# Every on-chip tile that a DMA reads or writes begins at a multiple of 256 bytes

## The chip, the core and the metric

The kernel runs on one core of one Trainium2 chip. The metric is the device time of one execution in microseconds (us). The kernel before takes 676.39 us, the median of three runs (676.08 to 677.17).

## What is computed

A hashed attention is followed by two dense expert layers. Each query and key falls into one of 64 buckets by the signs of six projections; a query sees only the keys of its own bucket.

```python
# q, k, v: [2, 8, 768, 64]; proj: [64, 6]
bucket = sum(((x @ proj) > 0) * 2**arange(6))           # for x = q and x = k
scores = where(q_bucket == k_bucket, q @ k.T / 8, -1e9)
attn   = softmax(scores) @ v                             # -> x: [1536, 512]
h = maximum(maximum(x @ w1, x @ w2), x @ w3)             # w1, w2, w3: [512, 768]
x = h @ w_out                                            # [768, 512]
g = x @ w_in                                             # [512, 2048]
out = where(g > 0, g, exp(minimum(g, 0)) - 1) @ w_out2   # [2048, 512]
```

Inputs and output are float32. TensorE multiplies float16 parts: each operand is split into a high and a low half, and a product is three matmuls (high by high, high by low, low by high).

## The kernel before

The work is cut into 24 units (two batches, three chunks of 256 queries, four pairs of heads), a unit into four tiles of 128 queries by 768 keys: 96 attention tiles. One tile goes through all engines. TensorE makes the scores (line 609), VectorE their row maximum (612), ScalarE the exponential into `P` (617), ScalarE, VectorE or GpSimd the high half and then GpSimd or VectorE the low half into `hl` (623, 625, 628). A DMA transpose from the SyncE queue turns `hl` into `PT` (630), 128 partitions of 1,536 elements of two bytes, and TensorE multiplies `PT` by the values (639 to 641). The result is divided, split into `xn` (661, 662) and transposed by another DMA into `xT` (665), from which the first expert layer starts. So each attention tile has one DMA transpose of 384 KB in its path, and there are 96 of them, with 12 smaller ones for `xT`.

Other DMAs load the inputs (`rawq`, `rawk`, `rawv`), the weights (`raww`, `raw2`) and store the output (`ot`); plain copies inside the chip bring half of the transposed queries and keys to other partitions (`qb<-qa`, `kb<-ka`, line 414) and add the bucket bits (`qb<-btq`, `kb<-btk`, line 461).

The order of the work is not found while the kernel runs. A graph of operations is built, and the string `ORDER` holds the sequence in which they are issued and the engine of each. Each engine executes its instructions in that sequence, and semaphores hold one back until its data are there. All tiles stand in pools that are laid out one after the other along the memory of a partition: `const`, `tiny` (small columns), `w13o` (weights of the first expert layer), `xp`, `hp`, `attn` (all tiles of the attention), and from the other end `wpre` (weights as loaded). When the attention is done its pool closes and `w2p` and `mp` (second expert layer) take its place; `x1p` takes that of `wpre`. Where a tile of a new pool lies over a tile of the old one, its first writer waits for the old tile's last user.

Where a tile begins is the sum of the sizes before it. The table in the section on the change gives the places.

Of the kernel before, what the change touches and what calls it, by code (L numbers as in the profile page):

```python
# [11 lines left out]
F32 = mybir.dt.float32  # L12
F16 = mybir.dt.float16
# [157 lines left out]
def lsh_attention_moe_kernel(ctx: ExitStack, tc: tile.TileContext, q, k, v, proj,  # L171
# [3 lines left out]
    NB = proj.shape[1]  # L175
# [11 lines left out]
    KM = DM // 128  # L187
    FM = DFF // 128
    F2 = DFF2 // 128
    NCH = B * NH  # L190
# [20 lines left out]
    const = ctx.enter_context(tc.tile_pool(name="const", bufs=1))  # L211
    tiny = ctx.enter_context(tc.tile_pool(name="tiny", bufs=2))
# [4 lines left out]
    at = g2.enter_context(tc.tile_pool(name="attn", bufs=1))  # L217
    gw = ctx.enter_context(ExitStack())
    wpre = gw.enter_context(tc.tile_pool(name="wpre", bufs=1, side="right"))
# [3 lines left out]
    late = {}  # L223
# [4 lines left out]
    def ring(pool, shape, tag, bufs, dt=F32, ordered=False):  # L228
        p = pool if callable(pool) else (lambda: pool)
        return g.buf(p, list(shape), dt, tag, bufs, ordered)  # L230

    def tn(n, tag, bufs, dt=F32):
        return ring(tiny, [128, n], tag, bufs, dt)
# [12 lines left out]
    tinyc = const.tile([128, 1], BF16, name="tinyc")  # L246
    flip = const.tile([128, 2], F32, name="flip")
    vts_ = [at.tile([128, 2, NS, VP], F16, name=f"vt{i}") for i in range(NP)]

    def emit_const():  # L250
        V.memset(ones, 1.0)
        V.memset(ones3, 1.03125)
        make_identity(nc, ident)
        A.activation(out=junk[:, 0:1], in_=ones[:, 0:1], func=AF.Square)

        V.memset(capc, 2.0 ** (2 * (62 + TQK - CAPQK) - 127 - 7))
        V.memset(pbt, 0.0)

        G.memset(tinyc, 2.0 ** -126)

        for j, (x, y) in enumerate(((1.0, -1.0), (0.0, 32768.0))):
            G.memset(flip[:, j:j + 1], x)
            G.affine_select(out=flip[:, j:j + 1], in_=flip[:, j:j + 1], compare_op=ALU.is_ge, fill=y,
                            base=QT * 4 * NB - 1, pattern=[[0, 1]], channel_multiplier=-1)

        for t in vts_:
            G.memset(t[:, :, :, D:D + 1], 1.0)
# [96 lines left out]
    def plan_qk(kind, b, p, hf, u, prio):  # L364
# [4 lines left out]
        nt = heads * n  # L369
# [3 lines left out]
        nb = QB if kind == "q" else NP  # L373
        raw = ring(at, [128, heads, n, D], "raw" + kind, 1 if kind == "q" else 2, ordered=True)
        nat = ring(at, [128, heads * n, 2, D], "nat" + kind, 1, F16, True)
        bits = ring(at, [128, NB * (2 if kind == "q" else 1), nt], "bits" + kind, 1, F16)
        ta = ring(at, [128, heads, n, 128], kind + "a", nb, F16, True)
        tb = ring(at, [128, heads, n, 128], kind + "b", nb, F16, True)
        acc, s, inv = tn(1, "acc" + kind, 2), tn(1, "s" + kind, 2), tn(1, "inv" + kind, nb + 1)
# [176 lines left out]
    w13 = wp.tile([128, FM, 3, 2, 512], F16, name="w13")  # L556
    wot = wp.tile([128, FM, 2, 512], F16, name="wot")
    swm = const.tile([128, 2, FM], F32, name="swm")
    osc = const.tile([128, 2], F32, name="osc")
    osm = const.tile([128, 2], F32, name="osm")  # L560
    omg = const.tile([128, 2], F32, name="omg")
    wosc = const.tile([128, FM], F32, name="wosc")
    wops = []

    def plan_w13(f, prio):
# [102 lines left out]


    x1T, x1acc, sx = {}, {}, {}  # L670

    def mm3(o, lh, rh, n):

        for kk in range(n):
            for pi, (x, y) in enumerate(((0, 0), (0, 1), (1, 0))):
                PE.matmul(o, lh(kk, x), rh(kk, y), start=(kk == 0 and pi == 0), stop=(kk == n - 1 and pi == 2))  # L676

    def plan_moe1(c, p0, dp):
# [32 lines left out]
        if c % 2 == 0:  # L711
            x1T[c // 2] = ring(lambda: late["x1p"], [128, KM, 2, 2 * NQ], "x1T", NCH // 2, F16)
        xs = slice(c % 2 * NQ, (c % 2 + 1) * NQ)
        x1acc[c] = const.tile([128, KM // 2], F32, name=f"x1acc{c}")
        sx[c] = const.tile([128, 2], F32, name=f"sx{c}")
        ch = tn(2, "ch", 2)
        pr = p0 + 18 * dp
        x2 = sumsq([bufcol(hacc, f) for f in range(FM // 2)], pr, also=[ch])
# [138 lines left out]
    for u in range(NU):  # L857
        c, p = divmod(u, NP)
        b, hf = divmod(c, NH)
        t0 = UL * u  # L860
        if hf == 0:
            plan_qk("k", b, p, hf, u, t0 - LQ)
        if p % 2 == 0:
            plan_qk("q", b, p, hf, u, t0 - LQ)
        if hf == 0:
            plan_v(b, p, t0 - LV)
        if u == NP - 1 or (hf == 0 and p == NP - 1):
            plan_vmin(b, t0 - LV)
# [20 lines left out]
            g.after(ld, sops[t])  # L889

    def close_w(e):
        gw.close()
        late["x1p"] = ctx.enter_context(tc.tile_pool(name="x1p", bufs=1, side="right", reuse_waits="tile"))

    g.after(op({"N": 0}, close_w, wr=["x1p"], prio=0.0 + 282.28), *wops)
    for c in range(NCH):
        if c % NH == 0:
            plan_sh(c // NH, (c + 1) * CS + LM + 18 * DM1)
        plan_moe1(c, (c + 1) * CS + LM + CM * c * 16, DM1)

    def close_attn(e):
        g2.close()
        late["w2p"] = ctx.enter_context(tc.tile_pool(name="w2p", bufs=1, side="right", reuse_waits="tile"))
        late["mp"] = ctx.enter_context(tc.tile_pool(name="mp", bufs=2, reuse_waits="tile"))
        late["ps_t"] = ctx.enter_context(tc.tile_pool(name="ps_t", bufs=1, space=PSUM, reuse_waits="tile"))
        late["ps_out"] = ctx.enter_context(tc.tile_pool(name="ps_out", bufs=2 * QT, space=PSUM, reuse_waits="tile"))

    g.after(op({"N": 0}, close_attn, wr=["w2p"], prio=0.0 + 767.79), *attn_ops)
    D2 = 51.9327
    M2 = NCH * CS + LM + 23 * DM1  # L910
    for c in range(NCH):
        plan_moe2_x(c, M2 - LM + c)
    f = 0
# [42 lines left out]
```

## Time and profile before

| | |
|---|---|
| median of 3 runs | 676.39 us |
| the profiled execution | 679.45 us |
| its span, first to last instruction | 677.6 us |
| TensorE matmuls busy | 621.6 us (92% of the span) |
| VectorE busy | 534.9 us (79%) |
| ScalarE busy | 443.5 us (65%) |
| GpSimd busy | 257.2 us (38%) |
| DMA packets | 201258, 167776 of them under 512 bytes |

Busy times are of one execution. The page cuts the span into 40 slices of 17 us; a digit is the busy share of a slice in tenths. The share of the DMA engines is the time of the packets that start in a stretch over 16 engines' time in it; packets overlap, so it can pass 100%.

### The profile page before, as it was taken

What the parts mean: (1) busy time and instruction counts of PE and PEld (TensorE: products, weight loads), DVE (VectorE), ACT (ScalarE), POOL (GpSimd) and SP (SyncE); (2) the same over time, 40 slices, a digit from 0 to 9 for tenths busy, and PEclk for the clock granted to TensorE, in tenths of its full rate; (3) what the DMA queues carried; (4) which work ended last, traced back from release to release, by engine and by line L of the source; (5) the groups of instructions that cost most, each with busy time, mean ns of one, the idle gap of its engine ahead of it and who ended that gap; (6) DMA issues with size and microseconds to landing.
All of it is one profiled execution on the core that took longest, in us unless ns stands there. A gap on an engine that the chain in (4) does not pass through costs nothing.

```text
span 677.6 us, 15392 instructions
## 1 busy us (share of the span) xinstructions
PE 621.6 (92%) x5838; PEld 421.2 (62%) x5838; DVE 534.9 (79%) x1478; ACT 443.5 (65%) x824; POOL 257.2 (38%) x244
## 2 busy tenths in 40 slices
PE   4776767999999999999999999999999999999997
PEld 4554446788878888777778886644444444444443
DVE  6898979999988778686965787877768887768655
ACT  4879977899677667767643688786665655633342
POOL 0344656476465556667542011133221112311111
PEclk9967657999999999999989999999999999999999
DMA  8999999999999977988977752321211000000003
GB/s 265 254 231 216 250 229 200 212 185 158 183 161 160 141 145 134 167 131 156 136 137 135 227 169 94 126 65 60 71 57 62 28 35 1 1 0 1 33 31 125
DMA packets 201258, 87.58 MB, mean 129 GB/s; under 512 B 167776, under 2 KB 195680, under 8 KB 201184
## 3 DMA queue, kind: packets, MB, share of 16 engines
q1 hardware_dynamic: 192810, 77.23, 55.8%
q10 hardware_dynamic: 8374, 9.37, 4.9%
q8 instruction: 46, 0.75, 0.5%
q14 instruction: 28, 0.23, 0.1%
HBM read 38.80 MB, written 3.15 MB: 62 GB/s over the span
## 4 chain that ended last, share of the span: by engine, by line
PE 62%; DMA 14%; DVE 9%; ACT 4%; issue 2%; POOL 2%; SPq 1%; ACTq 0%; DVEq 0%; POOLq 0%
PE mo L676 35%; PE out L804 18%; DMA PT<-hl 10%; PE s L609 4%; DMA raww<-in_moe_w_dram 2%; DVE m L612 2%; PE o L639 2%; PE o L640 1%; PE o L641 1%; ACT P L617 1%; POOL hl L628 1%; DVE hl L628 1%; DMA qb<-qa 1%; DMA rawq<-in_q_dram 1%; ACT hl L623 1%
## 5 line engine op out<-in xcount | busy, mean ns | idle before, releaser
L628 POOL TENSOR_TENSOR hl<-P,hl 128x768 f16<-128x768 f32 x78 | 132.8, 1707 | 97.4 <-ACT hl L623 45.1
L676 PE MATMUL mo<-xT,w 128*128 128x256 f16 x1296 | 151.5, 272 | 1.3 <-DVE invk L315 1.1
L676 PEld LDWEIGHTS <-w 128*128 128x128 f16 x1296 | 124.3, 98 | 19.2 <-issue 2.0
L804 PE MATMUL out<-wo2t,gt 128*128 128x512 f16 x576 | 131.9, 379 | 0.7 <-POOL gt L827 0.7
L676 PE MATMUL mo<-x1T,win 128*128 128x512 f16 x576 | 131.1, 379 | 0.5 <-DVE o2s L315 0.5
L617 ACT ACTIVATE P<-s,bias,scale 128x768 f32<-128x768 f32 x96 | 94.0, 987 | 38.2 <-DVE bias L615 18.5
L827 POOL TENSOR_TENSOR gt<-g,gt 128x256 f16<-128x256 f32 x57 | 39.3, 694 | 196.8 <-ACT gt L825 83.5
L612 DVE TENSOR_REDUCE m<-s 128x1 f32<-128x768 f32 x96 | 90.8, 951 | 23.4 <-PE s L609 20.4
L676 PEld LDWEIGHTS <-win 128*128 128x128 f16 x576 | 55.8, 98 | 67.2 <-issue 0.8
L804 PEld LDWEIGHTS <-gt 128*128 128x128 f16 x576 | 54.6, 97 | 64.2 <-POOL gt L827 1.5
L818 ACT ACTIVATE r<-mo,nih 128x256 f32<-128x256 f32 x96 | 43.7, 466 | 59.5 <-PE mo L676 53.0
L639 PE MATMUL o<-vt,PT 128*128 128x65 f16 x576 | 65.7, 199 | 12.6 <-DMA PT<-hl 10.6
L623 ACT CAST hl<-P 128x768 f16<-128x768 f32 x67 | 55.3, 827 | 26.3 <-DMA PT<-hl 22.1
L639 PEld LDWEIGHTS <-PT 128*128 128x128 f16 x576 | 56.0, 101 | 18.5 <-DMA PT<-hl 12.7
L640 PE MATMUL o<-vt,PT 128*128 128x64 f16 x576 | 65.5, 200 | 0.0
L641 PE MATMUL o<-vt,PT 128*128 128x65 f16 x576 | 65.3, 198 | 0.0
L609 PE MATMUL s<-ka,qa 128*128 128x384 f16 x192 | 52.6, 359 | 11.5 <-ACT P L617 11.3
L640 PEld LDWEIGHTS <-PT 128*128 128x128 f16 x576 | 56.0, 101 | 2.9 <-issue 1.0
L821 DVE TENSOR_SCALAR uu<-e,sg 128x256 f32<-128x256 f32 x96 | 36.7, 386 | 25.0 <-ACT e L820 24.6
L641 PEld LDWEIGHTS <-PT 128*128 128x128 f16 x576 | 56.0, 103 | 0.0
L609 PE MATMUL s<-kb,qb 76*128 76x384 f16 x192 | 53.3, 362 | 1.1 <-DMA kb<-btk 1.0
L823 DVE SCALAR_TENSOR_TENSOR g<-mo,aj,uu 128x256 f32<-128x256 f32 x96 | 45.6, 481 | 8.3 <-POOL gt L827 2.5
(207 smaller groups left out, 1102.7 us busy)
## 6 DMA issues: line engine op xcount, KB each, us to landing
raw<-in_moe_w_in_dram SPq DMA_DIRECT2D x14, 512.0 KB, 5.2
raw<-in_moe_w_out_dram SPq DMA_DIRECT2D x13, 512.0 KB, 3.9
raww<-in_moe_w_dram SPq DMA_DIRECT2D x11, 512.0 KB, 6.5
raww<-in_moe_w_dram ACTq DMA_DIRECT2D x7, 512.0 KB, 6.4
out_dram<-ot SPq DMA_DIRECT2D x11, 256.0 KB, 2.1
rawk<-in_k_dram SPq DMA_DIRECT2D x7, 384.0 KB, 3.3
rawv<-in_v_dram SPq DMA_DIRECT2D x7, 384.0 KB
rawq<-in_q_dram SPq DMA_DIRECT2D x10, 256.0 KB
```

The costliest lines, as they stand in the source:

```text
L609: PE.matmul(ps.ap[:, h, :NK], lh[0:n, h0 + i, j], rh[0:n, i, h * CH:(h + 1) * CH], start=first, stop=not first)
L612: op({"V": vred(S)}, lambda e: V.tensor_reduce(out=m.ap, in_=ps.ap[:, :, :NK], op=ALU.max, axis=AX.XY), rd=[ps], wr=[m], prio=t + 80.5)
L617: op({"A": act(S, ap=2) - 42}, lambda e: A.activation(out=P.ap.rearrange("p (c n) -> p c n", c=2), in_=ps.ap[:, :, :NK], func=AF.Exp, scal ...
L623: A.copy(hl.ap[:, 0], P.ap)
L628: op({"G": gtt(S), "V": (vtt(S), -109.46)}, lambda e: eng[e].tensor_tensor(out=hl.ap[:, 1], in0=P.ap, in1=hl.ap[:, 0], op=ALU.subtract), r ...
L639: PE.matmul(oo, pt.ap[:, kt], vt.ap[:, i, kt, :D + 1], start=(kt == 0), stop=False)
L640: PE.matmul(oo[:, :D], pt.ap[:, kt], vt.ap[:, i, kt, D + 2:], start=False, stop=False)
L641: PE.matmul(oo, pt.ap[:, NS + kt], vt.ap[:, i, kt, :D + 1], start=False, stop=(kt == NS - 1))
L676: PE.matmul(o, lh(kk, x), rh(kk, y), start=(kk == 0 and pi == 0), stop=(kk == n - 1 and pi == 2))
L804: PE.matmul(outs[z][j].ap, gt.ap[:, x, j * 128:(j + 1) * 128], wo2t[f].ap[:, y], start=(first and pi == 0), stop=(end and pi == 2))
L818: op({"A": act(NQ, ap=1) - 42}, lambda e, m=m, oz=oz, r=r, nih=nih: A.activation(out=r.ap, in_=oz(), func=AF.Relu, scale=nih.ap[:, m:m + 1 ...
L823: op({"V": vstt(NQ)}, lambda e, m=m, oz=oz, uu=uu, gg=gg, aj=aj: V.scalar_tensor_tensor(out=gg.ap, in0=oz(), scalar=aj.ap[:, m:m + 1], in1 ...
```

## The change

Six tiles are declared differently or added, all to shift what lies behind them; no operation is added, removed or moved, and the string `ORDER` is untouched.

```diff
     vts_ = [at.tile([128, 2, NS, VP], F16, name=f"vt{i}") for i in range(NP)]
+    const.tile([128, 32], F32, name="cpad")
...
-        bits = ring(at, [128, NB * (2 if kind == "q" else 1), nt], "bits" + kind, 1, F16)
+        bits = ring(tiny, [128, NB * (2 if kind == "q" else 1), nt], "bits" + kind, 1, F16)
...
-    osc = const.tile([128, 2], F32, name="osc")
-    osm = const.tile([128, 2], F32, name="osm")
-    omg = const.tile([128, 2], F32, name="omg")
-    wosc = const.tile([128, FM], F32, name="wosc")
+    o_ = const.tile([128, 6 + FM], F32, name="osc")
+    osc, osm, omg, wosc = o_[:, 0:2], o_[:, 2:4], o_[:, 4:6], o_[:, 6:]
...
+    x1a_ = const.tile([128, NCH, KM // 2], F32, name="x1acc")
+    sx_ = const.tile([128, NCH, 2], F32, name="sx")
...
-        x1acc[c] = const.tile([128, KM // 2], F32, name=f"x1acc{c}")
-        sx[c] = const.tile([128, 2], F32, name=f"sx{c}")
+        x1acc[c], sx[c] = x1a_[:, c], sx_[:, c]
...
     def close_w(e):
+        wpre.tile([128, 56], F32, name="wpad")
         gw.close()
...
     def close_attn(e):
+        late["x1p"].tile([128, 56], F32, name="xpad")
         g2.close()
```

The built programs give the start of each tile in its partition. As the remainder by 256 bytes:

| tiles | DMA's part in them | before | after |
|---|---|---|---|
| `hl`, `PT`, `xn` | source, destination, source of the transposes | 192 | 0 |
| `xT` | destination of the second kind of transpose | 96 | 0 |
| `qa0`, `qb0` | source and destination of a plain copy | 0 | 0 |
| `qa1`, `qb1`, `ka1` to `ka3`, `kb1` to `kb3`, all `bt` | the same | 192 | 0 |
| `ka0`, `kb0`, `rawq`, `rawk`, `rawv` | plain copy, loads | 96 | 0 |
| `raww`, `raw2` | loads of weights | 224 | 0 |
| `ot` | store of the output | 96 | 0 |
| `dc2`, `win`, `wo2t`, `x1T0`, `x1T1` | none | 224 | 0 |
| `w13`, `wot`, `hx`, `hT`, `g`, `gt` and the like | none | 96 | 0 |
| `vt` | none | 32 to 224 | 0 to 192 |

All starts are multiples of 32 bytes before and after. Of the twelve plain copies `qb<-qa` four stand in ScalarE's DMA queue: the first two copy `qa1` to `qb1`, the last two `qa0` to `qb0`.

The instructions of all five engines stand in the same order before and after, row for row. What differs are the waits of four rows of GpSimd, since tiles of the second expert layer now lie over other tiles of the attention. The names: `wo2t` and `win` are the split weights of that layer, `dc` the weights before the split, `gt` its activations, `x1T` its input, `hTb` a tile of the first layer. In brackets stand the engines and DMA queues for which a row waits.

GpSimd, the first weight of the second layer that it splits, before:

```order
L708 TENSOR_TENSOR hTb_7340<-hx_7273,hTb_7340 128x2x256 [waits DVE_49,PE_49]
L736 TENSOR_TENSOR x1T_7502<-hx_7426,x1T_7502 128x2x256 [waits DVE_49,Activation_49]
L546 TENSOR_SCALAR wo2t_7720<-dc_7355,o2s 128x512 [waits DVE_49,DMAHW6_49,PE_49,Pool_49]
L708 TENSOR_TENSOR hTb_7828<-hx_7677,hTb_7828 128x2x256 [waits DVE_49,Activation_49]
L827 TENSOR_TENSOR gt_7880<-g_7864,gt_7880 128x256 [waits Activation_49]
```

and now:

```order
L709 TENSOR_TENSOR hTb_7330<-hx_7263,hTb_7330 128x2x256 [waits DVE_49,PE_49]
L736 TENSOR_TENSOR x1T_7492<-hx_7416,x1T_7492 128x2x256 [waits DVE_49,Activation_49]
L547 TENSOR_SCALAR wo2t_7710<-dc_7345,o2s 128x512 [waits DMAHW6_49,DVE_49,Pool_49]
L709 TENSOR_TENSOR hTb_7818<-hx_7667,hTb_7818 128x2x256 [waits DVE_49,Activation_49]
L827 TENSOR_TENSOR gt_7870<-g_7854,gt_7870 128x256 [waits Activation_49]
```

The row of `wo2t` lost its wait for TensorE (PE); nothing moved.

GpSimd a little later, the next three weights, before:

```order
L546 TENSOR_SCALAR win_8352<-dc_7988,isc 128x512 [waits DMAHW0_49,DVE_49]
L736 TENSOR_TENSOR x1T_7502<-hx_8054,x1T_7502 128x2x256 [waits Activation_49]
L827 TENSOR_TENSOR gt_8399<-g_8354,gt_8399 128x256 [waits PE_49,Activation_49]
L827 TENSOR_TENSOR gt_8462<-g_8439,gt_8462 128x256 [waits Activation_49]
L827 TENSOR_TENSOR gt_8483<-g_8469,gt_8483 128x256 [waits PE_49,Activation_49]
L827 TENSOR_TENSOR gt_8530<-g_8528,gt_8530 128x256 [waits Activation_49]
L546 TENSOR_SCALAR wo2t_8537<-dc_7866,o2s 128x512 [waits DMAHW1_49]
L546 TENSOR_SCALAR win_8575<-dc_8139,isc 128x512
```

and now:

```order
L547 TENSOR_SCALAR win_8342<-dc_7978,isc 128x512 [waits DVE_49]
L736 TENSOR_TENSOR x1T_7492<-hx_8044,x1T_7492 128x2x256 [waits Activation_49]
L827 TENSOR_TENSOR gt_8389<-g_8344,gt_8389 128x256 [waits PE_49,Activation_49]
L827 TENSOR_TENSOR gt_8452<-g_8429,gt_8452 128x256 [waits Activation_49]
L827 TENSOR_TENSOR gt_8473<-g_8459,gt_8473 128x256 [waits PE_49,Activation_49]
L827 TENSOR_TENSOR gt_8520<-g_8518,gt_8520 128x256 [waits Activation_49]
L547 TENSOR_SCALAR wo2t_8527<-dc_7856,o2s 128x512 [waits DMAHW0_49]
L547 TENSOR_SCALAR win_8565<-dc_8129,isc 128x512 [waits DMAHW1_49]
```

The two waits for DMA queues went one weight further back; again nothing moved.

## Rows read from the trace of the kernel before

**Rows 1.** The page, busy tenths in 40 slices: TensorE and the DMA engines

```profile
PE   4776767999999999999999999999999999999997
DMA  8999999999999977988977752321211000000003
```

**Rows 2.** Busy time by stretch: us, each engine, granted clock, DMA share, GB/s

```profile
core 0: us, PE busy (x) PEld busy (x) DVE busy (x) ACT busy (x) POOL busy (x), PEclk, DMA share, GB/s
0.00:120.00 120.00, 81.56 (x983) 60.41 (x984) 103.27 (x288) 92.65 (x144) 52.65 (x48) 0.79 1.03 237
120.00:370.00 250.00, 237.94 (x3161) 201.06 (x3158) 200.91 (x491) 174.00 (x263) 145.56 (x125) 0.99 0.91 155
370.00:678.00 308.00, 302.06 (x1700) 159.69 (x1697) 230.77 (x701) 176.87 (x418) 58.98 (x71) 1.00 0.21 67
```

**Rows 3.** The chain that ended last: shares by line, then pieces (start us, us)

```profile
by line: PE mo L676 35.0%; PE out L804 17.6%; DMA PT<-hl 10.4%; PE s L609 4.0%; issue 2.2%; DMA raww<-in_moe_w_dram 1.7%; DVE m L612 1.7%; PE o L639 1.5%; PE o L640 1.3%; PE o L641 1.3%; ACT P L617 1.3%; POOL hl L628 0.9%; DVE hl L628 0.9%;
...
73.09 5.34 DMA PT<-hl
...
359.45 5.72 DMA PT<-hl
```

**Rows 4.** Waits in 120 to 370 us: us in total, times, longest us

```profile
PEld L639 <- DMA PT<-hl: 6.9, 8, 1.9
...
PE o L639 <- DMA PT<-hl: 5.5, 6, 1.8
```

**Rows 5.** DMA packets in 194.9 to 196.7 us, one transpose by itself

```profile
DMA packets 1498, 0.38 MB, mean 211 GB/s; under 512 B 1498, under 2 KB 1498, under 8 KB 1498
```

**Rows 6.** DMA packets in 128.3 to 129.6 us, a transpose that was held up

```profile
DMA packets 1475, 0.38 MB, mean 290 GB/s; under 512 B 1475, under 2 KB 1475, under 8 KB 1475
```

**Rows 7.** ScalarE's DMA queue in 38.8-39.7, 106.4-107.3, 169.3-171.2, 241.6-242.4 us: packets, MB, share

```profile
q10 hardware_dynamic: 79, 0.13, 40.5%
...
q10 hardware_dynamic: 79, 0.13, 66.8%
...
q10 hardware_dynamic: 79, 0.13, 26.4%
...
q10 hardware_dynamic: 72, 0.13, 63.7%
```

**Rows 8.** DMA packets in 4-8 us (loads), 373-376 us (loads), 661.9-664.1 us (stores)

```profile
DMA packets 1156, 1.36 MB, mean 340 GB/s; under 512 B 131, under 2 KB 1156, under 8 KB 1156
...
DMA packets 940, 1.12 MB, mean 374 GB/s; under 512 B 31, under 2 KB 882, under 8 KB 939
...
DMA packets 430, 0.79 MB, mean 358 GB/s; under 512 B 46, under 2 KB 46, under 8 KB 430
```

**Rows 9.** Last reader of PT, then GpSimd's timeline (start us, us, idle before)

```profile
L641 PE MATMUL o<-vt,PT x576: 191/192/247, 39.3 to 367.0; 128*128 128x65 f16 x192
...
398.97 1.59 POOL L546 TENSOR_SCALAR wo2t<-dc,o2s 128x512 f16<-128x512 f32 x1
...
444.31 1.66 POOL L546 TENSOR_SCALAR win<-dc,isc 128x512 f16<-128x512 f32 x1 [1.62 <-DVE cmi L774]
...
462.48 1.56 POOL L546 TENSOR_SCALAR win<-dc,isc 128x512 f16<-128x512 f32 x1
```

**Rows 10.** One operation on tiles at 96 and at 192: ns min/median/max

```profile
L827 POOL TENSOR_TENSOR gt<-g,gt x57: 666/671/1116, 415.1 to 669.1; 128x256 f16<-128x256 f32 x57
...
L662 POOL TENSOR_TENSOR xn<-xf,xn x19: 662/672/1315, 86.7 to 366.8; 128x256 f16<-128x256 f32 x19
```

**Rows 11.** Busy time in 340 to 344 us, columns as in Rows 2

```profile
340.00:344.00 4.00, 4.00 (x32) 2.95 (x29) 1.38 (x3) 0.39 (x2) 2.18 (x3) 0.57 0.78 120
```

**Rows 12.** Transposes from issue to landing, by the tile PT

```profile
DMA to landing us min/median/max: 3.7/4.8/6.6
```

## The prediction

> **What bounds the kernel now.** I read the page's busy tenths first, to see where TensorE is not full: its digits are 4 to 7 in the first seven slices and 9 nearly everywhere later, while the DMA line stays at 9 until about the middle [rows 1]. So the program has a first part in which many things limit each other and DMAs are always in flight, and a second in which TensorE alone counts. The busy times by stretch give sizes to that: in 0 to 120 us TensorE works 81.56 of 120, VectorE 103.27, and the DMA share is 1.03; in 120 to 370 us TensorE works 237.94 of 250 with a DMA share of 0.91; from 370 us on it is TensorE 302.06 of 308 at a DMA share of 0.21 [rows 2]. After 370 us there is no attention transpose any more and nothing that a faster DMA could shorten, except the last stores. What is open to a change of the DMAs is therefore the 38 us that TensorE idles before 120 us, most of which VectorE's load does not let go, and 12 us between 120 and 370.
>
> The chain that ended last says which DMA matters there: 35.0% is matmuls of line 676, and 10.4% is the attention's transposes from `hl` to `PT`; the next DMA, the first weights' loads, has 1.7% [rows 3]. The 10.4% are 70 us, in twelve pieces of more than 4 us, two of them before 120 us [rows 3]. A transpose lands 4.8 us after its issue in the median [rows 12]. TensorE itself waits little for it: in 120 to 370 us 5.5 us in 6 waits of matmuls and 6.9 us in 8 waits of weight loads [rows 4]; the rest of what the chain puts on transposes is covered by other work as soon as they are a little shorter.
>
> **The change part by part.** No instruction is added, removed or moved, so every term is the duration of something that is there before, at another address.
>
> The transposes come first. A transpose of 384 KB is 1,536 packets of 256 bytes; before, each reads at 192 and writes at 192 past a multiple of 256, so each crosses such a multiple on both sides; afterwards none does. The question is whether that crossing costs time now. A transpose that has the DMA engines to itself passes 1498 packets in 1.8 us [rows 5], that is 19.2 ns a packet on each of 16 engines, or 1.85 us in all. One that was held up first passes 1475 in 1.3 us [rows 6]: 14.1 ns a packet, 1.35 us in all. Both cross the same boundaries. So the engines can take crossing packets at 14.1 ns, and the 19.2 ns of the usual case must come from something else; I read it as the rate at which the packets are fed to the engines, since only the transpose that had time to be prepared runs faster. An aligned address does not feed them faster. I take no gain.
>
> The bounds: if the crossing were the reason after all, an aligned transpose would run at the held-up rate, 0.5 us shorter. Twelve pieces of the chain by 0.5 us are 6 us. For the other side there is a comparison inside the trace: the plain copies `qb<-qa` on ScalarE's queue, 64 packets of 2 KB each. The first two go between tiles at 192 and take 40.5% of 16 engines for 0.9 us, 5.8 us of engine time, and 66.8% of 0.9 us, 9.6 us; the last two go between tiles at 0 and take 26.4% of 1.9 us, 8.0 us, and 63.7% of 0.8 us, 8.2 us [rows 7]. The means are 7.7 us at 192 and 8.1 us at 0: the aligned copy is not cheaper, and 4.7% dearer within a spread that other transfers make. On 1.85 us that would be 0.09 us, times twelve 1.0 us. Between -6 and +1.0 I take 0, since the held-up transpose is the row nearest to it.
>
> [...]
>
> Loads and stores: they run at 340 GB/s in 4 to 8 us, when the first tiles are brought, at 374 GB/s in 373 to 376 us, and the stores of the output at 358 GB/s, all with unaligned tiles [rows 8]. If the beginning (4 to 12 us) ran at the best of these it would save a tenth of 8 us, 0.7 us; the 4.7% from above the other way are 0.4 us. I take 0, because the best row is itself unaligned.
>
> The waits of GpSimd: the first `wo2t` no longer waits for TensorE's last reader of `PT`. That was done at 367.0 us and the row starts at 398.97 [rows 9], so the wait never held. The `win` at 444.31 waited for VectorE, not for the DMA queue that is gone from its row; the later pair, whose DMA waits moved by one row, starts when the row before it ends [rows 9]. Nothing.
>
> The engines' own accesses: the same subtraction on GpSimd takes 671 ns in the median with tiles at 96 and 672 ns with tiles at 192 [rows 10]. The start does not show. The small tiles that are now columns of one share no new wait. Nothing.
>
> The sum is 0, with ends at -6.7 and +1.4. The profiled execution took 679.45 us with a span of 677.6; the median of the three runs is 3.1 us lower, and the sum carries over to it unchanged: 676.4 us. Small differences in landing shift a few tenths either way, and I say 676.3.
>
> **Rivals.** The first is that the crossing costs and the transposes become shorter by about 0.5 us. For it: DMA share near 1 over the whole attention [rows 2], and that no transpose ran aligned before. Against it: the held-up transpose [rows 6] and the copies [rows 7]. Of the 6 us the two pieces before 120 us would be lost to VectorE, which is busy 86% there; the ten after it give 5 us, and TensorE's own waits for transposes there, 5.5 us in 6 waits [rows 4], give back 3 us at once and the rest through ScalarE and VectorE in part. I put it at 4 us: 672.4. VectorE and GpSimd would then be late next. [...]
>
> [...]
>
> That the change does not do what it says is excluded: the built program has every tile that a DMA touches at a multiple of 256.
>
> **How the numbers follow.** No effect 0.53, shorter transposes (or a slow stretch less) 0.32, a slow stretch more 0.15. The likeliest case is 676.3 with its own range of 675.0 to 677.7. The range for eight in ten takes in most of the first rival, down to 671.8, and the second up to 678.2. By over 0.2% (1.35 us, about what a measurement can tell from no change) the time falls with 0.32, stays with 0.53 and rises with 0.15.
>
> **What would show it.** In the profile after, a transpose alone should still pass about 830 packets in a microsecond, and a held-up one about 1,130; from issue to landing should stay near 4.8 us; the chain should keep about a tenth on transposes; the DMA share in 120 to 370 us should stay near 0.9. If a transpose alone passes its packets at the held-up rate or faster, the first rival is right and my reading of the feed is wrong. [...]

## The result, and the profile after

The changed kernel takes 666.64 us, the median of four runs (664.99 to 668.42), beside 676.78 us for the kernel before (four runs, 676.08 to 678.92): a ratio of 0.9845 with a 95% interval of 0.9811 to 0.988. That is 10.1 us less, where no change was forecast. On two other chips, with more runs, the kernels whose source is aligned were 7.5 to 8.1 us faster (in the experiments), so 10.1 is the upper end of what was measured. The profiled execution took 666.32 us with a span of 664.5.

The page after, busy tenths of TensorE, its granted clock and the DMA engines, in 40 slices of 16.6 us:

```profile
PE   4777668999999999999999999999999999999997
...
PEclk9957777999999999999999999999999999999999
...
DMA  8999998987869967978878534222212100000003
```

The shape is that of [rows 1]; what differs is the DMA line, whose row of nines in the first half is broken, though as many bytes are moved (87.58 MB in both). The stretches of the kernel after, with the columns of [rows 2]:

```profile
0.00:120.00 120.00, 84.26 (x1013) 63.75 (x1014) 107.10 (x296) 95.61 (x149) 54.77 (x50) 0.82 1.00 243
120.00:370.00 250.00, 244.57 (x3256) 209.03 (x3254) 202.63 (x500) 177.73 (x273) 140.79 (x125) 1.00 0.82 165
...
340.00:344.00 4.00, 4.00 (x58) 3.46 (x55) 2.08 (x5) 2.79 (x4) 3.05 (x3) 1.00 0.50 114
```

In 120 to 370 us the DMA engines' share fell from 0.91 to 0.82 while they moved more per second (165 GB/s for 155). The last row stands against [rows 11]: the stretch at a granted clock of 0.57 is gone. The same work lies 9 to 13 us earlier now, but the clock is 1.00 in every 4 us from 320 to 344 us.

A transpose that has the engines to itself, and one that was held up, in the kernel after (230.4 to 231.7 us and 124.3 to 125.6 us):

```profile
DMA packets 1457, 0.37 MB, mean 283 GB/s; under 512 B 1457, under 2 KB 1457, under 8 KB 1457
...
DMA packets 1475, 0.38 MB, mean 289 GB/s; under 512 B 1475, under 2 KB 1475, under 8 KB 1475
```

The first now passes a packet every 14.3 ns on each of 16 engines (1.3 us by 16 over 1457), for 19.2 ns in [rows 5]; from its first packet to its last a transpose takes 1.52 us instead of 2.00. The held-up one is what it was in [rows 6]. From issue to landing, by the tile `PT`:

```profile
DMA to landing us min/median/max: 3.3/4.1/6.7
```

The median is 0.7 us below that of [rows 12]. The waits in 120 to 370 us, in total, times and longest; first a row of the kernel before that was not shown, ScalarE's write of `hl`:

```profile
ACT hl L623 <- DMA PT<-hl: 17.6, 16, 2.7
```

and after, the same wait and those that answer to [rows 4]:

```profile
ACT hl L622 <- DMA PT<-hl: 9.1, 7, 2.0
...
PEld L638 <- DMA PT<-hl: 2.7, 3, 1.4
...
PE o L638 <- DMA PT<-hl: 2.1, 2, 1.3
```

TensorE's waits of matmuls fell from 5.5 to 2.1 us, those of its weight loads from 6.9 to 2.7. ScalarE's fell from 17.6 to 9.1: it waits until a transpose has read the `hl` that it will overwrite, so a transpose holds up the front of the chain too.

**Where the 13 us of the two profiled executions lie.** The order is the same, so the same transposes can be found in both traces and the stretches between them compared. SyncE's timeline before (start us, us, number of transposes issued in a row):

```profile
122.19 11.11 SPq L630 DMA_TRANSPOSE PT<-hl  x4
...
154.77 5.11 SPq L630 DMA_TRANSPOSE PT<-hl  x3
...
248.96 15.43 SPq L630 DMA_TRANSPOSE PT<-hl  x6
...
304.67 25.12 SPq L630 DMA_TRANSPOSE PT<-hl  x9
```

and the same ones after:

```profile
118.78 10.39 SPq L629 DMA_TRANSPOSE PT<-hl  x4
...
150.25 4.53 SPq L629 DMA_TRANSPOSE PT<-hl  x3
...
244.49 14.19 SPq L629 DMA_TRANSPOSE PT<-hl  x6
...
295.36 24.73 SPq L629 DMA_TRANSPOSE PT<-hl  x9
```

Busy time in these stretches, and from the last of them to the last matmul that reads `PT` (367.0 us before [rows 9], 353.9 after), columns as in [rows 2]; before:

```profile
0.00:122.19 122.19, 83.75 (x1002) 62.18 (x1003) 105.46 (x291) 94.84 (x148) 54.32 (x50) 0.79 1.03 237
122.19:154.77 32.58, 30.90 (x429) 25.82 (x427) 30.58 (x84) 28.96 (x43) 19.87 (x14) 1.00 1.05 185
154.77:248.96 94.19, 91.86 (x1218) 78.64 (x1215) 80.17 (x208) 69.45 (x109) 54.54 (x44) 1.00 0.92 157
248.96:304.67 55.71, 51.62 (x699) 43.25 (x696) 42.61 (x98) 38.19 (x55) 36.63 (x35) 1.00 0.88 146
304.67:367.00 62.33, 58.37 (x779) 48.90 (x776) 42.78 (x92) 34.97 (x53) 32.37 (x34) 0.97 0.88 146
```

after:

```profile
0.00:118.78 118.78, 83.04 (x1002) 62.66 (x1003) 105.91 (x291) 94.46 (x148) 53.55 (x50) 0.81 0.99 245
118.78:150.25 31.47, 30.57 (x424) 25.75 (x422) 30.32 (x84) 28.66 (x43) 19.64 (x14) 1.00 1.00 188
150.25:244.49 94.24, 91.97 (x1223) 78.69 (x1220) 80.27 (x208) 69.63 (x109) 54.50 (x44) 1.00 0.80 157
244.49:295.36 50.87, 50.87 (x699) 43.17 (x696) 40.52 (x98) 39.00 (x56) 35.60 (x35) 1.00 0.80 163
295.36:353.90 58.54, 56.28 (x779) 48.07 (x776) 42.20 (x92) 34.16 (x52) 31.52 (x32) 1.00 0.82 153
```

The five stretches became shorter by 3.4, 1.1, -0.05, 4.8 and 3.8 us, 13.1 in sum, which is the whole difference of the spans (677.6 less 664.5). The third gives nothing: TensorE is busy 98% of it before and after. In the fourth TensorE's idle time fell from 4.1 us to nothing. In the fifth 1.7 us of the 3.8 are idle time, and the other 2.1 are the same 779 matmuls at a clock of 1.00 instead of 0.97. Over all five, TensorE's idle time fell by 9.3 us and its busy time by 3.8. What comes after the attention kept this lead, no more. The medians differ by 10.1 us; the profiled execution of before was 2.7 us above its median.

### The profile page after: what moved, and what is told of

The parts are those of the page before. It is cut to its first block, busy times and chain, and to the rows that moved or that the text cites. A ratio compares the mean times of both kernels' runs of the same rounds, so it can differ in the third digit from the quotient of the medians.

```text
span 664.5 us, 15390 instructions
## 1 busy us (share of the span) xinstructions
PE 617.8 (93%) x5838; PEld 420.7 (63%) x5838; DVE 532.5 (80%) x1478; ACT 443.5 (67%) x824; POOL 254.4 (38%) x244
## 2 busy tenths in 40 slices
DMA packets 201258, 87.58 MB, mean 132 GB/s; under 512 B 167776, under 2 KB 195680, under 8 KB 201184
## 4 chain that ended last, share of the span: by engine, by line
PE 59%; DVE 3%; DMA 2%; POOL 1%; ACT 1%; issue 1%; DVEq 0%; POOLq 0%; ACTq 0%
PE mo L677 34%; PE out L804 18%; PE s L608 3%; DMA PT<-hl 2%; PE o L638 1%; PE o L639 1%; PE o L640 1%; DVE m L611 1%; POOL hl L627 0%; ACT P L616 0%; DVE g L823 0%; DVE hl L627 0%; DVE xn L660 0%; POOL wo2t L547 0%; POOL win L547 0%
## 5 line engine op out<-in xcount | busy, mean ns | idle before, releaser
L638 PE MATMUL o<-vt,PT 128*128 128x65 f16 x576 | 66.6, 201 | 7.2 <-DMA PT<-hl 5.1
L640 PE MATMUL o<-vt,PT 128*128 128x65 f16 x576 | 66.2, 200 | 0.0
L638 PEld LDWEIGHTS <-PT 128*128 128x128 f16 x576 | 56.6, 102 | 12.8 <-DMA PT<-hl 6.9
L639 PEld LDWEIGHTS <-PT 128*128 128x128 f16 x576 | 56.6, 102 | 2.7 <-issue 0.9
L640 PEld LDWEIGHTS <-PT 128*128 128x128 f16 x576 | 56.7, 104 | 0.0
L608 PE MATMUL s<-kb,qb 76*128 76x384 f16 x192 | 51.9, 354 | 1.2 <-DMA kb<-btk 1.2
```

The source lines that it names most:

```text
L608: PE.matmul(ps.ap[:, h, :NK], lh[0:n, h0 + i, j], rh[0:n, i, h * CH:(h + 1) * CH], start=first, stop=not first)
L638: PE.matmul(oo, pt.ap[:, kt], vt.ap[:, i, kt, :D + 1], start=(kt == 0), stop=False)
L639: PE.matmul(oo[:, :D], pt.ap[:, kt], vt.ap[:, i, kt, D + 2:], start=False, stop=False)
L640: PE.matmul(oo, pt.ap[:, NS + kt], vt.ap[:, i, kt, :D + 1], start=False, stop=(kt == NS - 1))
```

## The experiments

Two theories at the start. A: a transpose whose packets cross a multiple of 256 bytes is slower for it, and that is the gain. B: the gain comes from elsewhere in the change, the changed waits of GpSimd or the engines' own accesses. Within A there were two questions: does the price grow with the bytes beyond the multiple, and is it paid on the read side, the write side or both. The packet rates below are always of one transpose alone on the engines, in 1.3 us, where nothing else is said.

**All tiles at 32 past a multiple.** The three pads of the change with other lengths, so that all else of the change stays:

```diff
-    const.tile([128, 32], F32, name="cpad")
+    const.tile([128, 40], F32, name="cpad")
...
-        wpre.tile([128, 56], F32, name="wpad")
+        wpre.tile([128, 48], F32, name="wpad")
...
-        late["x1p"].tile([128, 56], F32, name="xpad")
+        late["x1p"].tile([128, 48], F32, name="xpad")
```

> All tiles that start at 0 past a multiple of 256 in the changed kernel start at 32 past one instead; order and waits are those of the changed kernel. [...] Rival C (any crossing of a multiple of 256 costs the same, two parts instead of one): 211 GB/s and about 677. Rival L (not the crossing but where tiles lie over each other or over the pools): like the changed kernel, 283 GB/s and 667, since nothing but the start differs.

Measured: 676.58 us beside 675.71 for the kernel before on that chip, ratio 0.9989 (0.995 to 1.0027). The whole gain is gone with only the addresses changed, so the changed waits of GpSimd are not the cause, nor which tiles lie over each other (rival L). The engines' own accesses have moved with the tiles; they are compared further down, under the terms set to nothing. The transpose at 252.3 to 253.6 us:

```profile
DMA packets 1087, 0.28 MB, mean 214 GB/s; under 512 B 1087, under 2 KB 1087, under 8 KB 1087
```

The rate is that of [rows 5], though here only 32 of a packet's 256 bytes lie beyond the multiple. (The profiled execution of this kernel took 687.07 us, the longest of its eleven; only the rate is read from it.)

**All tiles at 224 past a multiple.** The first pad 96 bytes long, the others left out:

```diff
-    const.tile([128, 32], F32, name="cpad")
+    const.tile([128, 24], F32, name="cpad")
...
-        wpre.tile([128, 56], F32, name="wpad")
...
-        late["x1p"].tile([128, 56], F32, name="xpad")
```

> The same with 224 in place of 32. [...] Rival C: 211 GB/s and 677. Rival L: 283 GB/s and 667.

Measured: 676.39 us, ratio 1.0022 (0.9988 to 1.0055); at 196.1 to 197.4 us:

```profile
DMA packets 1083, 0.28 MB, mean 213 GB/s; under 512 B 1083, under 2 KB 1083, under 8 KB 1083
```

No dearer than 32: 213 GB/s beside 214. The price does not grow with the bytes beyond, so rival C stands; that a crossing packet goes in two parts, as its wording has it, no run shows.

**Only the source, or only the destination, at 192.** The tiles of the attention are reserved ahead in one list, with a pad of 192 bytes before the last kind; the two kernels differ in which kind is last, `hl` or `PT`. `raww` and `raw2` stand at 192 in both:

```diff
...
+    last = ['hl']
+    for tag in [t for t in sizes if t not in last] + ["pad"] + last:
+        if tag == "pad":
+            at.tile([128, 48], F32, name="apad")
+            continue
+        n, shape, dt = sizes[tag]
+        for j in range(n):
+            at.tile([128] + shape, dt, tag=f"{tag}{j}", name=f"{tag}{j}", bufs=1)
...
```

> Of the transposes' tiles only the source hl starts at 192, PT and the second kind's tiles stay at 0; the attention's tiles lie in another sequence, and the loaded weights, which need the room, are at 192 too. If the read side carries the price: a transpose alone at 211 GB/s and the kernel at 676 to 677. If the write side does: 283 GB/s and 667. If both share it: about 245 GB/s and 672.

> The counterpart: only the destination PT starts at 192, hl stays at 0, the loaded weights at 192 as in the kernel with the source at 192. If the read side carries the price: 283 GB/s for a transpose alone and 667. If the write side does: 211 GB/s and 676 to 677. If both share it: about 245 GB/s and 672. If instead loads into unaligned tiles cost time, both this kernel and its counterpart are slower than 667.

Measured, source at 192: 673.99 us, ratio 0.9979 (0.9935 to 1.0023), no gain that can be told. The transpose at 232.6 to 233.9 us:

```profile
DMA packets 1093, 0.28 MB, mean 215 GB/s; under 512 B 1093, under 2 KB 1093, under 8 KB 1093
```

Destination at 192: 667.61 us, ratio 0.9886 (0.9844 to 0.9927), the gain of the change within the intervals. At 232.9 to 234.2 us:

```profile
DMA packets 1459, 0.37 MB, mean 286 GB/s; under 512 B 1459, under 2 KB 1459, under 8 KB 1459
```

The price is on the read side alone (215 GB/s with the source at 192, 286 with the destination there). The weights as loaded stand at 192 in both, and the second takes 667.61 us all the same.

**The changed kernel again, and only the source at 0.** The first is the changed kernel without an edit, on the chip of the next two. In the second everything stands at 128 except `hl`, which is last behind a pad of 128 bytes, and the weights as loaded, which are at 0:

```diff
-    const.tile([128, 32], F32, name="cpad")
...
+    last = ['hl']
...
+            at.tile([128, 32], F32, name="apad")
...
```

> The changed kernel once more, beside the next two on one chip. Every theory: 0.985 of the kernel before, a transpose alone at 283 GB/s.

> The source hl alone starts at 0; PT, xn, xT and all tiles of the plain copies, the loads of q, k and v and the stores start at 128, loaded weights at 0. Theory S (only the read side of the attention's transposes costs, and one crossing costs the same at any start): a transpose alone at 283 GB/s and the whole gain, ratio 0.985 to 0.989. Rival M (the other tiles together give a part): a transpose alone at 283 GB/s but a ratio of 0.990 to 0.995. If only the pads' other effects counted: ratio 1.00.

Measured: the changed kernel 667.32 us beside 674.81, ratio 0.9886 (0.9838 to 0.9935); only the source at 0 666.99 us, ratio 0.9899 (0.9844 to 0.9953). The transpose of the latter at 241.4 to 242.7 us:

```profile
DMA packets 1456, 0.37 MB, mean 286 GB/s; under 512 B 1456, under 2 KB 1456, under 8 KB 1456
```

With `PT`, `xn`, `xT`, the copies' tiles, the inputs and the output unaligned, the gain of the changed kernel is there within the intervals. The address of `hl` is enough for it; that the other tiles add a small part (rival M begins at 0.990) is not excluded.

**One of three sources at 0.** `hl` has three buffers; here the first stands at 0, the others behind the pad at 192:

```diff
...
+            if tag == "hl" and j == 0:
+                at.tile([128, 48], F32, name="apad")
...
```

> One of the three buffers of hl starts at 0, two at 192, PT and the rest at 0, loaded weights at 192. Theory S with a gain in proportion to the transposes that are shorter: a third of the transposes alone take 1.5 us and two thirds 2.0 us, ratio about 0.995 (673 where the kernel before takes 676). Rival B (the slowest transposes set the pace, so that some shorter ones help nothing): ratio 1.00. Rival E (the first shorter ones remove the waits on the path and the others are hidden): ratio 0.987 to 0.990.

Measured: 670.94 us, ratio 0.9937 (0.9904 to 0.9969). Two neighbours in the trace, 315.7 to 317.0 us and 318.5 to 319.8 us:

```profile
DMA packets 1461, 0.37 MB, mean 286 GB/s; under 512 B 1461, under 2 KB 1461, under 8 KB 1461
...
DMA packets 1086, 0.28 MB, mean 214 GB/s; under 512 B 1086, under 2 KB 1086, under 8 KB 1086
```

The two rates stand side by side in one execution, so the rate belongs to the buffer. The gain is about half of the whole; a third (0.9962) lies inside the interval too, so how the gain adds up over the transposes is not settled.

**Transposes that are held up.** The kernel before, with two copies of `hl` to a scratch tensor queued ahead of every sixth transpose, to see whether being held up is what lets a crossing transpose pass fast. It adds 32 copies that nobody reads:

```diff
+        def turn_hl(e):
+            if t % 6 == 3:
+                for n in range(t // 6 * 2, t // 6 * 2 + 2):
+                    SP.dma_start(out=scr[n * 128:(n + 1) * 128, :], in_=hl.ap.rearrange("p t n -> p (t n)"))
+            SP.dma_start_transpose(out=pt.ap, in_=hl.ap.rearrange("p t n -> p (t n)"))
```

> The kernel before, unaligned, with two copies of hl to a scratch tensor issued ahead of every sixth attention transpose on the same queue; it does more work than the kernel before. Theory H (a crossing costs time only while the packets are still being fed to the engines; once they are prepared, 14.1 ns each in spite of it): the transposes right behind the copies take about 1.4 us from first to last packet, the others that run alone 2.0 us. Rival: the held-up transpose in the kernel before was fast for another reason, and those behind the copies take 2.0 us as well. The kernel takes 680 to 700.

Measured: 704.97 us in one run, above the 680 to 700 expected. First 155.8 to 157.1 us: the end of a transpose that had been held up (16 to 24 GB/s in 155.5 to 155.66 us), and the one behind it. Then one behind the copies (284.2 to 285.5) and one by itself (314.4 to 315.7):

```profile
DMA packets 1492, 0.37 MB, mean 288 GB/s; under 512 B 1492, under 2 KB 1492, under 8 KB 1492
...
DMA packets 1079, 0.27 MB, mean 211 GB/s; under 512 B 1079, under 2 KB 1079, under 8 KB 1079
...
DMA packets 1088, 0.28 MB, mean 214 GB/s; under 512 B 1088, under 2 KB 1088, under 8 KB 1088
```

Inconclusive. The transpose behind the copies ran as slowly as ever, 211 GB/s beside 214 by itself; the two copies took SyncE 0.80 to 1.00 us to issue in 90 to 180 us. The fast ones show again that crossing packets can pass at 288 GB/s, not what it takes.

The trace of the kernel before holds a nearer comparison, within one transpose. The one issued at 229.57 us stops partway, with 3 packets between 231.9 and 232.5 us. Its packets in 231.2 to 231.5 us, and in 232.9 to 233.6 us:

```profile
DMA packets 211, 0.05 MB, mean 178 GB/s; under 512 B 211, under 2 KB 211, under 8 KB 211
...
DMA packets 783, 0.20 MB, mean 286 GB/s; under 512 B 783, under 2 KB 783, under 8 KB 783
```

The address is the same on both sides of the stop, so the fast rate of crossing packets comes with the stop. Why is open.

**All tiles at 128, and all at 64.** Pads of other lengths, one run each. At 128 `cpad` is left out and

```diff
-        wpre.tile([128, 56], F32, name="wpad")
+        wpre.tile([128, 24], F32, name="wpad")
```

with `xpad` the same; at 64 they are 48 and 40 columns long.

> One look: all tiles that start at 0 in the changed kernel start at 128. If the boundary that counts is at 256 bytes, a transpose alone takes 2.0 us from first to last packet (211 GB/s) as at 32, 192 and 224. If it is at 128 bytes, 1.52 us (283 GB/s).

> One look: the same with 64. Boundary at 256 or 128 bytes: 2.0 us. At 64 bytes: 1.52 us, which the start at 192 of the kernel before already speaks against.

Measured: 673.97 us at 128 and 675.0 at 64, beside 677.39 for one run of the kernel before. One run each can't tell these from no change, since the kernel before alone spread over 9 us and more on the other chips; the rates can be told. At 128 (233.5 to 234.8 us):

```profile
DMA packets 1095, 0.28 MB, mean 216 GB/s; under 512 B 1095, under 2 KB 1095, under 8 KB 1095
```

and at 64 (246.1 to 247.4 us):

```profile
DMA packets 1094, 0.28 MB, mean 215 GB/s; under 512 B 1094, under 2 KB 1094, under 8 KB 1094
```

With 192 in the kernel before that makes five starts past a multiple, all at 211 to 216 GB/s, and 283 to 286 at the multiple itself.

**The same five stretches in these executions.** One pair of executions can't tell which of the differences between its stretches belong to the change. So here are the stretches between the same transposes in the other traces, on several chips. The source crosses in the kernel before, at 224, 192 (source only), 128 and 64, and is aligned in the changed kernel (twice), with the destination at 192 and with only the source at 0. The kernel at 32 (its execution was the long one) and the one with a third of the sources at 0 are left out.

| stretch | source crosses, us (mean of 5) | source aligned, us (mean of 4) | less |
|---|---|---|---|
| start to the issue near 122 us | 120.44 to 122.19 (121.47) | 118.78 to 121.64 (120.31) | 1.2 |
| second | 31.97 to 33.05 (32.57) | 31.11 to 32.03 (31.59) | 1.0 |
| third | 93.67 to 95.59 (94.46) | 93.05 to 94.30 (93.97) | 0.5 |
| fourth | 51.91 to 55.71 (53.28) | 50.75 to 52.56 (51.50) | 1.8 |
| fifth | 59.83 to 62.33 (60.77) | 58.39 to 59.26 (58.73) | 2.0 |

In sum 6.5 us, over half of it in the last two. The first stretch gave 1.2 us in the mean, not the 3.4 of the one pair. The ranges of the first four stretches overlap, those of the fifth do not. The clock of the fifth is 0.97 in the kernel before and with only the source at 192 (62.33 and 61.88 us), but 1.00 in the other three crossing kernels (59.83 to 59.93) and in all four aligned ones.

## Why the prediction was wrong

**The step that failed** is "So the engines can take crossing packets at 14.1 ns, and the 19.2 ns of the usual case must come from something else". The first half is true and still is: [rows 6] are not disproved. The second half does not follow. An aligned transpose by itself runs at 283 GB/s (14.3 ns a packet), so whatever feeds the packets was not the limit at 211; and the same kernel with only the addresses moved goes back to 213 to 216. That an aligned address does not feed the packets faster was my assumption; no row showed it. Crossing is what makes a lone transpose slow, by the same at each of the five starts and on the source's side alone, under a condition that a held-up one does not meet (290 GB/s in [rows 6]). I took one fast row as proof that the address is free, where it only showed that the price is not always paid. The bound of 0.5 us that I worked out beside it was the right one: 2.00 less 1.52 us.

**The rival that came true** is the first, and it was sized too small: 4 us, against 10.1 in the first comparison and 7.5 to 8.1 on the other chips. Its two pieces before 120 us were to be lost to VectorE, but the first stretch became 1.2 us shorter in the mean. The stretches behind it give 5.3 us, more than the 4 that I took. In the pair of profiled executions a landing became 0.7 us shorter in the median, not 0.5, and TensorE's idle time fell by 9.3 us, where I let its own waits give back "3 us at once and the rest through ScalarE and VectorE in part". ScalarE's waits for `hl` in 120 to 370 us fell from 17.6 to 9.1 us there; they are 12.1 to 17.6 us in the five crossing executions and 8.7 to 11.7 in the four aligned ones. I read this as many transposes late by a little each, which hold up the engine that refills their source and which a count of the chain's pieces above 4 us misses; the runs do not separate these terms.

**The clock.** The stretch at 0.57 went. Its 4.00 us of matmuls at that clock [rows 11] are by estimate 1.7 us of work lost (4.00 by 0.43), and the fifth pair of stretches shows 2.1 us less for the same matmuls. The crossing alone does not make that stretch, since three crossing kernels have a clock of 1.00 there. So some 2 of the 13.1 us between the two profiled executions lie in a slow stretch that some kernels with a crossing source have and others have not; whether shorter transposes make it rarer is open. That twelve landings 0.7 us shorter, 8.4 us, and these 1.7 add up to 10.1 is coincidence.

**A slow stretch more**, to which the prediction gives 0.15 and the end of its range at 678.2, did not occur: the clock of 120 to 370 us rose from 0.99 to 1.00. No run shows that term, or what brings such a stretch about; what the runs showed in its place is a stretch less.

**The terms that I set to nothing** hold within the intervals. Stores, copies, the other transposes, all destinations and the loads of the inputs are unaligned in the kernel with only the source at 0, and the loads of the weights in the one with only the destination at 192; both are as fast as the changed one (ratios of 0.9899 and 0.9886 to the kernel before, beside its 0.9886). The copies of [rows 7] were rightly read as showing no gain, but their packets are of 2 KB, and they did not speak for a transpose's packets of 256 bytes. GpSimd's rows after:

```profile
L547 POOL TENSOR_SCALAR wo2t<-dc,o2s x2: 1592/1596/1599, 385.9 to 447.8; 128x512 f16<-128x512 f32 x2
...
L827 POOL TENSOR_TENSOR gt<-g,gt x57: 666/672/1112, 402.1 to 656.0; 128x256 f16<-128x256 f32 x57
...
L661 POOL TENSOR_TENSOR xn<-xf,xn x19: 658/670/1316, 84.3 to 354.2; 128x256 f16<-128x256 f32 x19
```

The first `wo2t` starts 13.1 us earlier than in [rows 9], which is the lead that the attention gave and nothing more: the wait that it lost never held. The subtractions take 672 and 670 ns, as in [rows 10]. The engines' writes of `hl`, the tile whose address counts, did not change either; ScalarE's, before and after:

```profile
L623 ACT CAST hl<-P x67: 802/831/851, 30.3 to 358.8; 128x768 f16<-128x768 f32 x67
...
L622 ACT CAST hl<-P x67: 804/832/853, 30.7 to 345.8; 128x768 f16<-128x768 f32 x67
```

GpSimd's subtraction into it takes 1646 ns in the median both times, VectorE's 956 and 955. So it is the transposes' reading of `hl` that became faster, not its writing.

**What the profile was to show.** Packets of a lone transpose at the held-up rate was named as the sign of the first rival, and it came. From issue to landing did not stay near 4.8 us, nor the DMA share near 0.9. The chain can't be set against [rows 3], since after it is followed back only to about 216 us:

```profile
PE 59%; DVE 3%; DMA 2%; POOL 1%; ACT 1%; issue 1%; DVEq 0%; POOLq 0%; ACTq 0%
```

Its shares add up to 67%, so the 2% of DMAs are not what is left of the 10.4%.

## What to carry to other kernels

Where a DMA transpose of 256-byte packets reads from on-chip memory, let its source tile begin at a multiple of 256 bytes: a transpose took 1.52 us here instead of 2.00. One pad is enough (with only the source at 0 the kernel was 7.8 us faster), and the destination cost nothing at 128 or 192 (286 GB/s each). When one row shows that a price is sometimes not paid, don't strike it out: ask under what condition, and give the rival that it speaks against a chance to match. Where two traces differ in many stretches, look at the same stretches in further executions before giving each a cause. To size the gain of a shorter transfer, compare stretches between the same transfers and read the waits of the engine that refills its source, not only of the one that reads its result.

## What the runs showed of the hardware

- A lone transpose of 384 KB passes at 211 to 216 GB/s with its source at 32, 64, 128, 192 or 224 past a multiple of 256 bytes (2.00 us from first to last packet in the kernel before, at 192) and at 283 to 286 GB/s at the multiple (1.52 us in the changed kernel). The first 32 bytes across cost as much as 224: 214 and 213 GB/s.
- The destination's address shows no price: with `PT` at 192, and with `PT` at 128, a transpose alone passes at 286 GB/s, and the gain is there within the intervals.
- A transpose that was held up passed at 290 GB/s with a crossing source in the kernel before and at 288 in the one with the added copies, beside 289 in the changed kernel, and one that stopped partway in the kernel before went on at 286 GB/s after 178 before the stop; why is open.
